# Reordering the first 16 microseconds: weight pieces between the input loads, an eviction moved up, a variance moved down

## The chip, the cores and the metric

The kernel runs on one core of one Trainium2 chip. The metric is device time in microseconds (us) of one execution; several executions give a median. Most executions of one kernel here agree within 0.3%, about 2.4 us. The change is about fractions of a microsecond at the very start of an 802 us kernel; the traces stamp each instruction to about 0.01 us. "Span" is the time from the first to the last instruction in a profiled execution; it is some 2 us shorter than the device time.

## The reference, cut to what matters

```python
def reference(A_x, A_wq, A_wk, A_wv, A_wo, A_beta, B_x, B_w_in, B_w_sp, B_b_sp, B_w_out):
    h = x + _A_ref(_layernorm(x), A_wq, A_wk, A_wv, A_wo, A_beta)   # segmented attention with a memory
    return h + _B_ref(_layernorm(h), B_w_in, B_w_sp, B_b_sp, B_w_out)  # gated MLP
```

x is 2048 x 1024 in bf16. The sequence is worked on in four segments of 512 tokens, each segment in four chunks of 128. Only the start matters here: the layernorm of the first segment's four chunks (0 to 3), their transposition, and the first projections with w_v, w_k and w_q.

## The kernel before: the parts that the change and the argument touch

All instructions go through a recorder that keeps the written order on each engine and sets the semaphores. So the order of the lines is the order on each engine.

For the first segment, only the mean is subtracted before the transposition. 1/std is applied later: to V when it leaves PSUM, where TensorE puts its results (`v_out`; such a copy out of PSUM is called an eviction), and to Q and K through a row vector RB, which TensorE makes with two matmuls of ones x diag(1/std). Those two matmuls need the 1/std of all four chunks. Variances come either from VectorE's statistics (chunks 0, 1, 2) or from a ScalarE pass over squares (chunk 3, `act_var`).

```python
    for tc in range(4):
        x_load(tc)
    for i in range(0, 8, 2):                      # w_v's first half in four pieces of 256 KB
        sp.dma_start(WV[0][:, i:i + 2, :], A_wv[...])
    sp.dma_start(WK[:, :, 0:256], ...)            # then w_k, beta, w_q, w_v's second half
    ...
    def act_mean(tc):    # ScalarE: MEAN[tc] = -sum(x) / D
    def act_var(tc):     # ScalarE: sum of (x - mean)^2; GpSimd adds eps
    def var0(k):         # GpSimd: variance from VectorE's statistics, plus eps
    def rstd0(tc):       # GpSimd: RS0[tc] = var ** -0.5
    def center(tc, m):   # VectorE: x - mean, in bf16
    def diag(tc):        # VectorE: two operations, diag(RS0[tc]) as a bf16 pair
    def pe_Th(tcl, src, e0, e1):  # TensorE: 8 transposes into 2 PSUM banks, evicted by engines e0 and e1
    ...
    warm(9)
    act_mean(1)
    var0(ln_stats(XCH[0]))
    c0 = center(0, MV[0][:, 0:1], ALU.subtract)
    c1 = center(1, MEAN[1][:])
    pe_Th(0, c0, dve, dve)
    act_mean(2)
    pe_Th(1, c1, act, dve)
    act_mean(3)
    rstd0(0)
    c2 = center(2, MEAN[2][:])
    var0(ln_stats(XCH[1]))
    rstd0(1)
    act_var(3)
    c3 = center(3, MEAN[3][:])
    warm(2)
    vb = [next_bank() for _ in range(2)]
    for i in range(5):
        for t in range(2):
            v_mm(0, t, 0, vb[t], i)      # V of chunks 0 and 1: needs chunk 0 and 1 transposed, and w_v
    pe_Th(2, c2, act, dve)
    rstd0(3)
    var0(ln_stats(XCH[2]))
    rstd0(2)
    diag(0)
    for i in range(5, 8):
        for t in range(2):
            v_mm(0, t, 0, vb[t], i)
    pe_Th(3, c3, act, dve)
    v_out(0, 0, 0, vb[0]); diag(1); diag(3); diag(2); v_out(0, 1, 0, vb[1])
    proj_v(0, 2, 0)
    ...
    mm8(bank(bk), WK ..., XNT[0] ...)             # first w_k projection
    for i in range(2):
        pe.matmul(bank(br), ONES[:], DIAG[i]...)  # ones x diag
    mm8(bank(bq), WQ ..., XNT[0] ...)             # first w_q projection
    for tc in range(4, 8):
        x_load(tc)
    sp.dma_start(WK[:, :, 256:D], ...)            # 1.5 MB
    sp.dma_start(WQ[:, :, 256:D], ...)            # 1.5 MB
    phi_exp(0); phi_max(0)                        # ends with the first transposed load, pk<-pqk
    ...
    def state(n):                                 # matmuls PK x V; state(0) needs the first pk
```

The softmax here doesn't subtract the row's maximum and nothing guards it: scores larger than these inputs give would overflow.

## Time and profile before

| | before |
|---|---|
| device time, median of 3 (range) | 802.45 us (801.4 to 803.39) |
| span of the profiled execution | 800.7 us |
| TensorE busy | 789.3 us (99%) |
| first w_v piece landed | 8.37 us |
| first w_q weight load | 16.52 us |

A page line "PE 789.3 (99%)" says that hardly anything is to be gained outside the places where TensorE stands still. These places are at the start. The next lines are from the timeline of the kernel before, TensorE's weight loads (PEld; PE are its matmuls, DVE is VectorE, ACT ScalarE, POOL GpSimd). The columns are start, time taken, engine, line, operation, out<-in, shapes and count; the brackets say how long the engine had idled and what ended it. I read weight loads rather than matmuls, since some matmul records are missing (this trace holds 15 of the first 16 V matmuls). A weight load starts up to 0.2 us ahead of its matmul: here transposes 3 are at 12.19 and 12.41.

```profile
5.79 0.90 PEld L209 LDWEIGHTS ps<-ident,lno 128*128 128x128 bf16 x16 [1.10 <-DVE lno L209]
...
8.48 1.85 PEld L209 LDWEIGHTS ps<-wv,xnT 128*128 128x128 bf16 x10 [1.68 <-DVE lno L209]
...
12.19 0.65 PEld L209 LDWEIGHTS ps<-ident,lno 128*128 128x128 bf16 x8
12.80 1.45 PEld L209 LDWEIGHTS ps<-wv,xnT 128*128 128x128 bf16 x8
14.37 1.61 PEld L209 LDWEIGHTS ps<-xnT,wk 128*128 128x128 bf16 x8
16.09 0.31 PEld L209 LDWEIGHTS ps<-diag,ones 128*128 128x128 bf16 x2
16.52 0.53 PEld L209 LDWEIGHTS ps<-xnT,wq 128*128 128x128 bf16 x3
```

No weight was loaded for 1.7 us ahead of the first V matmul at 8.48 (TensorE itself, which still worked on the two warm-up matmuls, stood for 1.2 us of that). The transposes of chunk 3 started at 12.19. From there to the first w_q weight load at 16.52, which I call "the tail", there is no bracket: TensorE was never held up. The tail is 16.52 - 12.19 = 4.33 us. The name in the 1.68 us bracket (DVE lno) is not the true releaser: lno was long written. The chain of waits of the same kernel (start, time taken, what) names it, and also shows what came next:

```profile
2.65 5.72 DMA wv<-in_A_wv_dram
8.37 0.14 issue
8.51 3.63 PE ps L209 x22
12.14 0.05 issue
12.19 8.30 PE ps L209 x44
20.49 10.24 DMA pk<-pqk
30.73 0.05 issue
30.78 0.41 PE ps L209 x4
```

TensorE waited for the w_v piece until 8.37, and the `state(0)` matmuls at 30.78 began as soon as pk had landed at 30.73. VectorE's timeline of the kernel before shows where the statistics of chunk 2 and the diag operations lay:

```profile
11.65 1.41 DVE L209 BATCH_NORM_STATS2 stats<-xch 128x6 f32<-128x512 bf16 x2
...
13.73 0.42 DVE L209 COPY xnT<-ps 128x512 bf16<-128x512 bf16 x1
...
15.46 0.35 DVE L209 SCALAR_TENSOR_TENSOR diag<-ident,rs,diag 128x128 bf16<-128x128 bf16 x1
```

The statistics ran ahead of chunk 3's copy (13.73), and the last diag operation ended at 15.81, before TensorE asked for it at 16.09.

### The profile page before, as it was taken

The page shows a single profiled execution, that of the slowest core. Times are in us where ns is not written, and L with a number is a line of the kernel's source. Part 1 is how long each engine was busy: PE and PEld are TensorE (multiplying, and loading weights), DVE is VectorE, ACT ScalarE, POOL GpSimd, SP SyncE. Part 2 cuts the span into 40 slices and gives each one's busy share as a digit, 9 for nine tenths or more (in the row PEclk, how much of TensorE's full clock was granted, in tenths as well). Part 3 has the DMA queues.
Part 4 walks back from the last instruction along what each step waited for, and adds up shares of the span by engine and source line. Part 5 has one row for each costly group of instructions (what it writes and reads, how often), then busy time and mean ns, then how long its engine had stood idle before and what let it go on. Part 6 is the DMA issues. An engine that isn't in the chain of part 4 may idle for free.

```text
span 800.7 us, 12419 instructions
## 1 busy us (share of the span) xinstructions
PE 789.3 (99%) x5301; PEld 380.0 (47%) x5371; DVE 379.2 (47%) x769; ACT 297.9 (37%) x347; POOL 129.0 (16%) x241
## 2 busy tenths in 40 slices
PE   8999999999999999999999999999999999999998
PEld 3445445555454445455544444444444444444444
DVE  6675688569853774844562000053234323323432
ACT  5777877877778675133333333100000000000000
POOL 4443333333333331100131000000000000000000
PEclk9999999999999999999999999999999999999999
DMA  9772535353516324611116000650270153021002
GB/s 292 176 164 56 93 81 119 87 102 83 99 31 126 113 54 100 170 47 53 53 53 132 1 0 1 203 107 6 80 132 1 33 110 75 0 66 47 1 7 86
DMA packets 125000, 64.79 MB, mean 81 GB/s; under 512 B 94992, under 2 KB 113936, under 8 KB 124944
## 3 DMA queue, kind: packets, MB, share of 16 engines
q1 hardware_dynamic: 124944, 63.99, 33.6%
q8 instruction: 42, 0.69, 0.4%
q14 instruction: 14, 0.11, 0.1%
HBM read 32.51 MB, written 8.39 MB: 51 GB/s over the span
## 4 chain that ended last, share of the span: by engine, by line
PE 94%; DVE 3%; DMA 2%; issue 1%; SPq 0%
PE ps L209 94%; DMA pk<-pqk 1%; DMA wv<-in_A_wv_dram 1%; DVE stats L209 1%; DVE ta L209 0%; DVE otok L209 0%; DVE hch L209 0%; SPq L209 0%; DVE rd L209 0%; DVE pqk L209 0%; DVE mzb L209 0%; DVE lno L209 0%; DVE rdm L209 0%; DVE msum L209 0%; DVE mv L209 0%
## 5 line engine op out<-in xcount | busy, mean ns | idle before, releaser
L209 PE MATMUL ps<-wspT,z 128*128 128x512 bf16 x878 | 193.1, 379 | 0.9
L209 ACT ACTIVATE e<-ps 128x2048 bf16<-128x2048 f32 (+1 forms) x96 | 152.8, 1592 | 49.5 <-PE ps L209 49.0
L209 PEld LDWEIGHTS ps<-wspT,z 128*128 128x128 bf16 x896 | 87.7, 98 | 105.7
L209 DVE TENSOR_TENSOR tmpg<-ps,brow 128x512 f32<-128x512 f32 x56 | 38.7, 691 | 197.0 <-DMA brow<-in_B_b_sp_dram 105.5
L209 POOL TENSOR_SCALAR_AFFINE_SELECT e<-e 128x512 bf16<-128x512 bf16 x128 | 83.9, 666 | 179.9 <-ACT e L209 179.8
L209 PE MATMUL ps<-win,hnT 128*128 128x448 bf16 x512 | 98.3, 352 | 0.0
L209 PE MATMUL ps<-w_out,yT 128*128 128x512 bf16 (+2 forms) x453 | 96.9, 372 | 0.5
L209 PE MATMUL ps<-hnT,win 128*128 128x512 bf16 x439 | 96.2, 379 | 0.5
L209 PEld LDWEIGHTS ps<-win,hnT 128*128 128x128 bf16 x512 | 49.8, 98 | 46.3 <-issue 0.2
L209 PEld LDWEIGHTS ps<-w_out,yT 128*128 128x128 bf16 x462 | 44.7, 98 | 52.4
L209 PEld LDWEIGHTS ps<-hnT,win 128*128 128x128 bf16 x448 | 43.9, 98 | 52.8
L209 PE MATMUL ps<-xnT,wk 128*128 128x512 bf16 x256 | 60.8, 380 | 0.0
L209 PE MATMUL ps<-wv,xnT 128*128 128x512 bf16 x254 | 58.8, 379 | 1.3 <-DMA wv<-in_A_wv_dram 1.2
L209 ACT ACTIVATE z<-ps 128x448 bf16<-128x448 f32 x60 | 32.5, 543 | 69.4 <-PE ps L209 69.4
L209 PE MATMUL ps<-wo,oT 128*128 128x512 bf16 x254 | 57.6, 379 | 0.1
L209 ACT ACTIVATE z1T<-ps 128x512 bf16<-128x512 f32 x56 | 33.4, 597 | 63.3 <-PE ps L209 63.3
L209 DVE TENSOR_TENSOR fin<-fin,ps 128x512 bf16<-128x512 bf16 (+2 forms) x33 | 22.2, 672 | 71.2 <-DMA fin<-out_dram 40.0
L209 PE MATMUL ps<-xnT,wq 128*128 128x512 bf16 x226 | 54.0, 379 | 1.6
L209 DVE BATCH_NORM_STATS2 zst<-z 128x6 f32<-128x448 bf16 x64 | 38.9, 620 | 30.1 <-ACT z L209 30.1
L209 PEld LDWEIGHTS ps<-v,e 128*128 128x128 bf16 x1280 | 37.3, 96 | 9.1 <-issue 1.7
L209 DVE TENSOR_TENSOR yT<-tmpg,z1T 128x512 bf16<-128x512 f32 x56 | 38.8, 692 | 1.9
L209 PE MATMUL ps<-v,e 128*128 128x33 bf16 x1280 | 38.4, 177 | 0.0
(83 smaller groups left out, 574.0 us busy)
## 6 DMA issues: line engine op xcount, KB each, us to landing
xch<-in_A_x_dram SPq DMA_DIRECT2D x16, 256.0 KB, 3.2
xr<-in_A_x_dram SPq DMA_DIRECT2D x16, 256.0 KB, 3.6
out_dram<-hch SPq DMA_DIRECT2D x16, 256.0 KB, 2.5
fin<-out_dram SPq DMA_DIRECT2D x16, 256.0 KB, 2.8
out_dram<-fin SPq DMA_DIRECT2D x31, 128.0 KB, 1.7
win<-in_B_w_in_dram SPq DMA_DIRECT2D x4, 896.0 KB, 5.3
w_out<-in_B_w_out_dram SPq DMA_DIRECT2D x1, 3584.0 KB, 13.6
win<-in_B_w_in_dram SPq DMA_DIRECT2D x3, 1024.0 KB, 5.4
```

Of the source, the lines that this page charges most:

```text
L209: ins = getattr(e, op.name)(*op.args, **op.kw)
```

## The change

The intent is to let the V matmuls start earlier. w_v's pieces come between the x chunks; ScalarE evicts chunk 1 before it works on chunk 2's mean; the two warm-up matmuls that filled the wait go. In exchange, chunk 3's variance (ScalarE) and, with it, chunk 2's statistics (VectorE) move behind chunk 3's transposes. The centering of chunk 2 (`c2`) also moves, behind chunk 1's statistics on VectorE.

```diff
-    for tc in range(4):
-        x_load(tc)
-    for i in range(0, 8, 2):
-        sp.dma_start(WV[0][:, i:i + 2, :],
-                     A_wv[i * 128:(i + 2) * 128, 0:512].rearrange("(c p) n -> p c n", p=128))
+    for k in range(8):
+        if k in (0, 1, 3, 5):
+            x_load((k + 1) // 2)
+        else:
+            i = {2: 0, 4: 2, 6: 4, 7: 6}[k]
+            sp.dma_start(WV[0][:, i:i + 2, :],
+                         A_wv[i * 128:(i + 2) * 128, 0:512].rearrange("(c p) n -> p c n", p=128))
@@
     pe_Th(0, c0, dve, dve)
+    pe_Th(1, c1, act, dve)
     act_mean(2)
-    pe_Th(1, c1, act, dve)
-    act_mean(3)
     rstd0(0)
-    c2 = center(2, MEAN[2][:])
     var0(ln_stats(XCH[1]))
     rstd0(1)
-    act_var(3)
-    c3 = center(3, MEAN[3][:])
-    warm(2)
+    c2 = center(2, MEAN[2][:])
+    act_mean(3)
     vb = [next_bank() for _ in range(2)]
-    for i in range(5):
+    for i in range(4):
         for t in range(2):
             v_mm(0, t, 0, vb[t], i)
     pe_Th(2, c2, act, dve)
+    c3 = center(3, MEAN[3][:])
+    for i in range(4, 8):
+        for t in range(2):
+            v_mm(0, t, 0, vb[t], i)
+    pe_Th(3, c3, act, dve)
+    act_var(3)
     rstd0(3)
     var0(ln_stats(XCH[2]))
     rstd0(2)
     diag(0)
-    for i in range(5, 8):
-        for t in range(2):
-            v_mm(0, t, 0, vb[t], i)
-    pe_Th(3, c3, act, dve)
     v_out(0, 0, 0, vb[0])
```

## The prediction

> **What bounds it.** Over the 800.7 us span TensorE is busy 99% (the page's part 1). The change touches the first 15 us alone. By the timeline, TensorE there waits until 5.80 us for the first transposes, and from 7.29 to 8.51 for the first w_v piece (the chain of waits: 5.72 us of "DMA wv", then TensorE until 20.49). Then the chain leaves TensorE: "DMA pk<-pqk" from 20.49 to 30.73, the transposed load that the first `state` matmuls wait for; they start at 30.78, when TensorE's previous work (logits) has just ended at 30.65. So TensorE has only some 0.1 us of slack against that landing.
>
> **What moves, costed from the trace.**
> Landings go by slot of 256 KB: 3.5, 4.2, 6.3, 7.7, 8.4, 9.1, 9.9 and 10.6 us. The Trainium skill (DMA: Bandwidth & Descriptors, "Queues, rings and completion order") says each engine consumes descriptors in ring order; the landings agree. The new order gives w_v piece 0 the 6.3 slot instead of 8.4, x2 7.7 instead of 6.3, piece 1 8.4, x3 9.1, pieces 2 and 3 still 9.9 and 10.6.
>
> - Chunk 1's ScalarE eviction (0.58 us) no longer stands behind mean 2 (1.06 + 0.19): it ends near 7.1 instead of 8.0. Two warm matmuls go.
> - V matmuls (0.22 us each) start near 7.2 instead of 8.5, stall about 0.3 us for piece 1, end their first eight near 9.3. Mean 2 runs 7.7–9.0, c2 ends 9.45; transposes 2 near 9.5; the next eight 9.9–11.65; transposes 3 11.65–12.1 instead of 12.4–12.85. `proj_v(0,2)` starts 0.75 us earlier, the w_k projection too, ending near 15.6 instead of 16.3.
> - But now variance 3 comes late: ScalarE does it after chunk 3's eviction, about 12.5–13.8 (before: 9.1–10.3), and VectorE's statistics of chunk 2 (1.41 + 0.21) stand behind chunk 3's copy, 12.5–14.1. GpSimd then makes the two rstd one after the other (0.2 + 0.6 each), ending near 15.6; the last diag pair ends near 16.2 (before 15.8). The ones×diag matmuls, which started at 16.31, will wait for it, and start at about 16.25. So nearly all of the 0.75 us is given back there: instead of a wait for w_v, a wait of about 0.6 us for diag.
>
> **On the critical path.** At the ones×diag matmuls I expect 0 to 0.2 us gain (a loss of up to 0.4 is possible). Anything that remains ends at `state(0)`: the pk landing hangs behind w_k and w_q (3 MB), in a stream that runs at 350–390 GB/s from 14 to 26 us (the same page puts the HBM limit of a core near 358; the trace is slightly above it). The same bytes go out in the same time, so pk lands near 30.7 whatever TensorE did before. Net effect: about 0.
>
> **Predicted:** 802.5 us, range 801.3 to 803.6 (8 in 10; mostly the spread of the runs, 801.4 to 803.4). Chances: faster by over 2% 0.005, within 2% 0.985, slower by over 2% 0.01.
>
> **Would show it right:** first V matmul at 7.1–7.5 us; transposes 3 at 11.5–12; a new TensorE wait of about 0.6 us on DVE diag before the ones×diag matmuls, which start at 16.1–16.5; `state(0)` at 30.6–30.9, with TensorE's part of the wait on DMA pk unchanged or slightly longer; the rest of the trace shifted by less than 0.3 us.
>
> **Would make it wrong:** the dip of the load stream at 3.5–5 us (74–213 GB/s) vanishing or growing with the new order, which would move all landings, pk too; GpSimd's rstd ops faster or slower than 0.6 us; w_v piece 0 or x2 landing over 1 us off their slots; x loads 6 and 7, which now wait for later readers, delaying w_k and w_q so far that the stream runs dry.

## The result, and the profile after

| | before | after |
|---|---|---|
| device time, median of 4 (range) | 802.57 us (801.4 to 803.39) | 802.28 us (801.98 to 802.58) |
| ratio, 95% interval | | 0.9997 (0.998 to 1.0015) |
| span of the profiled execution | 800.66 us | 800.25 us |
| first w_v piece landed | 8.37 us | 5.99 us |
| transposes of chunk 3 | 12.19 us | 11.21 us |
| first w_q weight load | 16.52 us | 16.30 us |
| first pk landed | 30.73 us | 29.62 us |

A ratio is the mean time of one kernel's fast runs over that of the other's fast runs of the same rounds, so it is not quite the ratio of the medians. The timeline of the kernel after, weight loads, answers the lines of before:

```profile
6.64 0.10 PEld L209 LDWEIGHTS ps<-wv,xnT 128*128 128x128 bf16 x1
7.25 0.33 PEld L209 LDWEIGHTS ps<-wv,xnT 128*128 128x128 bf16 x3 [0.52 <-ACT xnT L209]
...
9.23 0.45 PEld L209 LDWEIGHTS ps<-ident,lno 128*128 128x128 bf16 x8 [0.78 <-DVE lno L209]
...
11.21 0.65 PEld L209 LDWEIGHTS ps<-ident,lno 128*128 128x128 bf16 x8
11.81 1.45 PEld L209 LDWEIGHTS ps<-wv,xnT 128*128 128x128 bf16 x8
13.38 1.61 PEld L209 LDWEIGHTS ps<-xnT,wk 128*128 128x128 bf16 x8
15.89 0.10 PEld L209 LDWEIGHTS ps<-diag,ones 128*128 128x128 bf16 x1 [0.91 <-DVE diag L209]
16.28 0.10 PEld L209 LDWEIGHTS ps<-diag,ones 128*128 128x128 bf16 x1 [0.29 <-DVE diag L209]
16.30 0.75 PEld L209 LDWEIGHTS ps<-xnT,wq 128*128 128x128 bf16 x4
```

The V matmuls start at 6.64 instead of 8.48, 1.84 us earlier, and the transposes of chunk 3 are 0.98 us earlier. Much of the difference is the wait of 0.78 us at 9.23: the transposes of chunk 2 now wait for VectorE, which centers chunk 2 behind chunk 1's statistics. No run moved that operation back. But the tail now has a wait in it, named DVE diag, and takes 16.30 - 11.21 = 5.09 us instead of 4.33. So 0.76 of the 0.98 us are given back. VectorE's timeline of the kernel after shows what the wait is made of:

```profile
12.07 0.42 DVE L209 COPY xnT<-ps 128x512 bf16<-128x512 bf16 x1 [1.35 <-PE ps L209]
12.41 1.41 DVE L209 BATCH_NORM_STATS2 stats<-xch 128x6 f32<-128x512 bf16 x2
13.86 0.21 DVE L209 BATCH_NORM_AGGREGATE mv<-stats 128x2 f32<-128x12 f32 x1
13.98 0.20 DVE L209 TENSOR_SCALAR diag<-ident,rs 128x128 bf16<-128x128 bf16 x1
...
15.88 0.35 DVE L209 SCALAR_TENSOR_TENSOR diag<-ident,rs,diag 128x128 bf16<-128x128 bf16 x1
```

VectorE idles 1.35 us ahead of chunk 3's copy. Only then come the statistics (1.6 us with the aggregate) and the eight diag operations (2.25 us), one after the other without a gap, to 16.23.

The weight loads of `state(0)` (first line before, second after; each from its own timeline) answer to the chain's pk step:

```profile
30.78 0.23 PEld L209 LDWEIGHTS ps<-v,pk 128*128 128x128 bf16 x4 [0.41 <-DMA pk<-pqk]
```

```profile
30.35 0.23 PEld L209 LDWEIGHTS ps<-v,pk 128*128 128x128 bf16 x4 [0.21 <-issue]
```

After, pk landed 1.1 us earlier and nothing waited for it. I had said that it would land at the same time.

### The profile page after: what moved, and what is told of

Read it like the earlier page. It is cut to its first block, busy times and chain, and to the rows that moved or that the text cites. A ratio compares the mean times of both kernels' runs of the same rounds, so it can differ in the third digit from the quotient of the medians.

```text
span 800.3 us, 12483 instructions
## 1 busy us (share of the span) xinstructions
PE 793.6 (99%) x5369; PEld 379.8 (47%) x5369; DVE 379.5 (47%) x769; ACT 297.9 (37%) x347; POOL 129.2 (16%) x241
## 4 chain that ended last, share of the span: by engine, by line
PE 95%; DVE 4%; ACT 0%; issue 0%
PE ps L209 95%; DVE stats L209 1%; ACT e L209 0%; DVE ta L209 0%; DVE otok L209 0%; DVE hch L209 0%; DVE diag L209 0%; DVE rd L209 0%; DVE xnT L209 0%; DVE pqk L209 0%; DVE lno L209 0%; DVE mv L209 0%; DVE mzb L209 0%; DVE etmp L209 0%; DVE rdm L209 0%
## 5 line engine op out<-in xcount | busy, mean ns | idle before, releaser
L209 PE MATMUL ps<-xnT,wq 128*128 128x512 bf16 x256 | 60.5, 379 | 0.0
```

Of the source, the lines that this page charges most:

```text
L209: ins = getattr(e, op.name)(*op.args, **op.kw)
```

## The experiments

Twelve runs were made: eight (a profile and one time each) and five rounds of four kernels. All results were correct. Here is what all fourteen traces show. Times are us from the start of the span; the transposes, w_q and `state(0)` are the starts of their weight loads; "tail" is w_q minus transposes 3; "clock" is the moment from which the trace's clock record has TensorE's full clock; "rest" is span minus w_q.

| run | loads / engines | clock | w_v piece landed | transposes 3 | w_q | tail | pk landed | state(0) | span | rest |
|---|---|---|---|---|---|---|---|---|---|---|
| before | old / old | 4.47 | 8.37 | 12.19 | 16.52 | 4.33 | 30.73 | 30.78 | 800.66 | 784.14 |
| b_rep | old / old | 5.52 | 7.64 | 11.46 | 15.79 | 4.33 | 29.78 | 29.84 | 799.70 | 783.91 |
| b_r5 | old / old | 5.25 | 7.40 | 11.27 | 15.60 | 4.33 | 29.74 | 29.78 | 799.67 | 784.08 |
| after | new / new | 5.86 | 5.99 | 11.21 | 16.30 | 5.09 | 29.62 | 30.35 | 800.25 | 783.96 |
| a_rep | new / new | 4.62 | 6.63 | 11.35 | 16.43 | 5.08 | 29.18 | 30.49 | 800.35 | 783.92 |
| a_r5 | new / new | 5.89 | 6.27 | 11.33 | 16.42 | 5.09 | 29.07 | 30.48 | 800.36 | 783.94 |
| loads_only | new / old | 5.30 | 5.84 | 12.12 | 16.45 | 4.33 | 28.74 | 30.51 | 800.38 | 783.93 |
| engines_only | old / new | 6.41 | 7.83 | 11.65 | 16.74 | 5.09 | 29.07 | 30.80 | 800.66 | 783.92 |
| a_var3 | new / new, variance 3 early | 5.07 | 5.01 | 11.41 | 16.50 | 5.09 | 28.65 | 30.56 | 800.42 | 783.92 |
| a_stats2 | new / new, statistics 2 early | 5.07 | 5.64 | 11.21 | 16.33 | 5.12 | 30.41 | 30.46 | 800.35 | 784.02 |
| a_both | new / new, both early | 5.84 | 5.55 | 11.24 | 15.57 | 4.33 | 29.75 | 29.79 | 799.66 | 784.09 |
| a_both_r5 | the same | 6.82 | 6.17 | 11.70 | 16.03 | 4.33 | 29.43 | 30.08 | 799.98 | 783.95 |
| a_both_pk | both early, pk before w_q's rest | 7.45 | 5.73 | 12.03 | 16.36 | 4.33 | 24.51 | 30.42 | 800.29 | 783.93 |
| a_both_pk_r5 | the same | 4.46 | 5.92 | 11.30 | 15.63 | 4.33 | 24.87 | 29.69 | 799.75 | 784.12 |

The last column is the key to the table. Behind the first w_q matmul all kernels are alike: 783.91 to 783.96 us, or up to 0.2 us more where something still held TensorE near `state(0)`. So span = transposes 3 + tail + rest, and each of the three terms can be looked at alone.

### The kernel before, again (b_rep)

Its edit is nothing: it asks how far the trace of before repeats.

> The kernel before, unchanged, for the scatter of single stamps. If traces repeat: first V matmul 8.5 us, transposes of chunk 3 at 12.4, ones x diag at 16.3, first w_q matmul 16.7 (each within 0.15), w_q's rest lands at 29.5 and the first pk at 30.7, state(0) at 30.8. Theory A (the 0.2 us at state(0) is a wait on pk that lands late because of the load order): pk again after 30.5. Rival B (pk's landing varies by a us from run to run, whatever the order): pk may land anywhere from 29.5 to 31, and state(0) then starts at 30.6 without a wait in some runs.

Measured: 801.42 us (before on the same chip: 802.26), span 799.70. It did not repeat. The w_v piece landed at 7.64, and everything behind it was 0.73 us earlier up to w_q. The timeline, weight loads:

```profile
7.75 1.85 PEld L209 LDWEIGHTS ps<-wv,xnT 128*128 128x128 bf16 x10 [0.87 <-DVE xnT L209]
...
11.46 0.65 PEld L209 LDWEIGHTS ps<-ident,lno 128*128 128x128 bf16 x8
...
15.79 1.18 PEld L209 LDWEIGHTS ps<-xnT,wq 128*128 128x128 bf16 x6
```

and the step of its chain of waits that stands where before had 5.72 us:

```profile
2.65 4.99 DMA wv<-in_A_wv_dram
```

The same load, issued at the same moment, took 4.99 instead of 5.72 us. Between 4 and 5 us the load stream moved 152 GB/s in the first profile of before and 254 in this one (windows view). So the trace that I had predicted from held a slow draw of a load, and the size of the possible gain was read from that draw. Theory A, that the load order fixes pk's landing, also fell here: pk landed at 29.78 with the old order.

### The changed kernel, again (a_rep)

> The changed kernel, unchanged, for the scatter. If traces repeat: first V matmul 6.6 us, transposes of chunk 3 at 11.4, ones x diag 15.9, first w_q matmul 16.5, state(0) 30.4. Theory A: pk lands again near 29.6, before TensorE needs it. Rival B: it may land as late as 30.7, and state(0) then waits until then.

Measured: 802.06 us, span 800.35. This one repeats: w_q at 16.43 against 16.30, although the piece landed 0.64 us later than in the first trace. The V matmuls start at 6.78 and 6.64: set by the transposes, not by the load. pk landed at 29.18 and was not waited for.

### The new loads alone (loads_only)

```diff
 before, with the new order of the eight loads; the engines' order is untouched
```

> Only the new order of loads; all engines in the order of before. First V piece lands near 6.0, x2 near 6.8 (0.5 later than before). ScalarE still does mean 2 before chunk 1's eviction, so that ends near 8.6 and the V matmuls start near 8.7, 0.2 later than before: the piece that landed early is of no use. My theory (TensorE's start is set by the later of piece and eviction, so both parts of the change are needed): transposes of chunk 3 at 12.5-12.8, first w_q matmul 16.7-17.0. Rival (the loads alone bring the gain): V matmuls before 7.7 and w_q before 16.5. Theory A of pk: pk lands near 29.6 as in the changed kernel; rival B: no telling.

Measured: 802.10 us, span 800.38. The piece landed at 5.84, but only the first V matmul used it. Its timeline, weight loads:

```profile
6.77 0.10 PEld L209 LDWEIGHTS ps<-wv,xnT 128*128 128x128 bf16 x1
8.64 1.62 PEld L209 LDWEIGHTS ps<-wv,xnT 128*128 128x128 bf16 x9 [1.77 <-ACT xnT L209]
```

The second V matmul needs chunk 1, which ScalarE still evicts behind mean 2; it waited until 8.64 for it. The expectation for that (near 8.7) was right. The expected stamps are those of matmuls: transposes 3 were expected at 12.5 or later and started at 12.34, the first w_q matmul at 16.7 or later and started at 16.67. The rival's w_q before 16.5 did not come. Of the V matmuls, which it had before 7.7, only the first started so early. Against the two repeats of before, w_q is 0.66 and 0.85 us later. So the loads alone bring nothing, and against a quick draw of before they cost.

### The new engine order alone (engines_only)

```diff
 after, with the old order of the eight loads
```

> Only the new order on the engines; loads as before. Chunk 1 is evicted by 7.2, but the V matmuls wait for the first piece until about 8.4-8.5. Then eight matmuls, transposes 2 near 10.3, transposes 3 near 12.4, and behind them variance 3 (to 14.5), statistics of chunk 2 (to 15), diag (to 17.2): ones x diag at 16.9, first w_q matmul at 17.4-17.6, that is 0.7-0.8 later than before, and state(0) near 31.4. Rival (the late variance and statistics cost nothing, as TensorE has other work): w_q at 16.7 or earlier. Theory A of pk: pk lands near 30.7 with the old loads, too early to matter here.

Measured: 802.38 us, span 800.66. The piece landed at 7.83, earlier than the 8.4 to 8.5 that I had counted on, and the absolute times are earlier by about as much (first w_q matmul 16.95 instead of 17.4 to 17.6). Against its own transposes the result is clear:

```profile
11.65 0.65 PEld L209 LDWEIGHTS ps<-ident,lno 128*128 128x128 bf16 x8
...
16.34 0.10 PEld L209 LDWEIGHTS ps<-diag,ones 128*128 128x128 bf16 x1 [0.90 <-DVE diag L209]
```

The tail is 5.09 us, as in the changed kernel, and has the same wait. In b_rep and here transposes 3 start 3.82 us after the piece has landed, so with the landing taken out the new engine order costs the tail's 0.76 us and gains nothing by itself. Only with both parts do transposes 3 stop following the landing: in after, a_rep and a_r5 they start at 11.21 to 11.35, with the piece landing at 5.99 to 6.63.

### Which of the two moved operations makes the wait (a_var3, a_stats2, a_both)

The changed kernel is edited in three ways: variance 3 alone put ahead of chunk 3's transposes, statistics 2 alone, and both.

```diff
-    pe_Th(3, c3, act, dve)
     act_var(3)
     rstd0(3)
+    pe_Th(3, c3, act, dve)          # a_var3
     var0(ln_stats(XCH[2]))
```

```diff
+    k2 = ln_stats(XCH[2])           # a_stats2
     pe_Th(3, c3, act, dve)
     act_var(3)
     rstd0(3)
-    var0(ln_stats(XCH[2]))
+    var0(k2)
```

a_both has `act_var(3); rstd0(3); k2 = ln_stats(XCH[2])` ahead of `pe_Th(3, ...)`.

> The changed kernel with variance 3 put back ahead of chunk 3's eviction (ScalarE is idle from 10.3 to 11.8 there, and it takes 1.24 us). Theory C (the diag chain is held at two places at once: VectorE's statistics of chunk 2 behind chunk 3's copy, and variance 3): no gain from this alone, since VectorE still reaches diag 0 at 14.0 and ends the eight diag operations at 16.2: ones x diag at 15.9, w_q at 16.5, both within 0.1 of the changed kernel. Rival D (the late variance is the whole cost, as the change's words suggest): ones x diag at 15.3, w_q at 15.75.

> The changed kernel with the statistics of chunk 2 put ahead of chunk 3's copy on VectorE (idle there from 10.7 to 12.1; they take 1.63 us, so the copy comes 0.25 later). Theory C: no gain from this alone either: diag 0 and 1 are done by 13.9, but diag 3 waits for variance 3 (rstd ready near 14.5) and diag 2 for the rstd that GpSimd makes after it (15.5): ones x diag near 15.9, w_q 16.4-16.6. Rival E (VectorE's statistics are the whole cost): ones x diag at 15.3, w_q at 15.75.

> Both moves. Theory C: the wait on diag is gone, w_k's projection runs straight into ones x diag at 15.3 and w_q at 15.75, 0.75 earlier than the changed kernel and 1.0 than before. state(0) would be free at 29.6. If pk lands at 29.6 as in the changed kernel it starts at 29.6-29.8; if pk's landing is set by the load stream and lies at 30.7, it starts there and 1 us of the gain is lost (theory of my prediction). Rival F (the w_k and w_q pieces or something else holds TensorE there too): w_q at 16.3 or later with another engine or a load named in the wait.

Measured: a_var3 802.14 us, tail 5.09; a_stats2 802.07 us, tail 5.12; a_both 801.38 us, tail 4.33. Either move alone gains nothing, both together gain the whole 0.76 us. The two rivals that blamed one operation fell. In a_var3 VectorE still works from 12.61 to 16.43 without a gap. In a_stats2 VectorE is early and waits for GpSimd instead, whose 1/std of chunks 3 and 2 stand behind the late variance. VectorE's timeline of a_stats2:

```profile
13.33 0.35 DVE L209 SCALAR_TENSOR_TENSOR diag<-ident,rs,diag 128x128 bf16<-128x128 bf16 x1
14.52 0.25 DVE L209 TENSOR_SCALAR diag<-ident,rs 128x128 bf16<-128x128 bf16 x1 [0.84 <-POOL rs L209]
...
15.62 0.26 DVE L209 TENSOR_SCALAR diag<-ident,rs 128x128 bf16<-128x128 bf16 x1 [0.46 <-POOL rs L209]
```

Two chains end at the same moment, and each covers the other. In a_both VectorE's idle time ahead of chunk 3's copy is filled with the statistics (10.66 to 12.32), and no line has a bracket. VectorE's statistics and copy, then TensorE's weight loads, of a_both:

```profile
10.66 1.42 DVE L209 BATCH_NORM_STATS2 stats<-xch 128x6 f32<-128x512 bf16 x2
...
12.24 0.37 DVE L209 COPY xnT<-ps 128x512 bf16<-128x512 bf16 x1
```

```profile
11.24 0.65 PEld L209 LDWEIGHTS ps<-ident,lno 128*128 128x128 bf16 x8
...
15.14 0.31 PEld L209 LDWEIGHTS ps<-diag,ones 128*128 128x128 bf16 x2
15.57 1.39 PEld L209 LDWEIGHTS ps<-xnT,wq 128*128 128x128 bf16 x7
```

The first w_q matmul, some 0.2 us behind its weight load, started at 15.79; 15.75 was expected. At `state(0)` pk landed at 29.75 and held TensorE for about 0.17 us (rest 784.09 against 783.92). So a kernel that is early enough does meet pk, as b_r5 does too (784.08).

### pk ahead of w_q's remainder (a_both_pk)

```diff
-    sp.dma_start(WQ[:, :, 256:D], wcols(A_wq, 256, D))
     phi_exp(0)
     phi_max(0)                       # issues the transposed load of pk
+    sp.dma_start(WQ[:, :, 256:D], wcols(A_wq, 256, D))
```

> Both moves, and the load of w_q's remaining 1.5 MB issued after the first transposed load of pk and not before it. If pk queues behind those bytes (1.5 MB at about 370 GB/s is 4.1 us, an estimate), it lands near 25-26.5 instead of 29.6-30.7, and state(0) starts at 29.6 without a wait. The rest of w_q then lands near 29.5-30.5, and its first use (third head group, near 30) may wait for it: up to 0.5 us. Rival (pk's landing has another cause, such as the transposed mode itself): still 29.5 or later.

Measured: pk landed at 24.51 instead of 29.75, w_q's remainder at 28.73, and `state(0)` did not wait. That pk queues behind those 1.5 MB is shown. Here is the load of pk in the two kernels' DMA views (kind, count, us from issue to landing), before first, then a_both_pk:

```profile
pk<-pqk SPq DMA_TRANSPOSE x1, 10.2
```

```profile
pk<-pqk SPq DMA_TRANSPOSE x1, 4.2
```

But the execution was slow at another place: 802.00 us, w_q at 16.36. Its 16 first transposes took 1.85 us. Here are the TensorE lines of the two executions of this one kernel, a_both_pk first, then a_both_pk_r5:

```profile
5.77 1.85 PE L209 MATMUL ps<-ident,lno 128*128 128x128 bf16 x16 [0.15 <-DVE lno L209]
```

```profile
5.82 1.07 PE L209 MATMUL ps<-ident,lno 128*128 128x128 bf16 x16 [0.71 <-DVE lno L209]
```

In the first the clock record shows TensorE's full clock only from 7.45 us on, in the second from 4.46. The Trainium skill (TensorE: Matmul & The Clock Gate, "Part 1: The HAM clock gate") says that the array runs at half clock until a free-running window has seen enough activity, and calls the moment run-variable. The traces agree that the moment varies; the window itself no run here shows. The same code differs by 0.78 us in these transposes, which start 0.106 us apart in the first and 0.056 us apart in the second, and by 0.73 us at transposes 3 (12.03 against 11.30). In a_both_r5 the full clock came at 6.82 and transposes 3 start at 11.70, against 11.24 in a_both. With the old loads such a delay can hide behind the wait for the piece: in engines_only the full clock came at 6.41, and transposes 3 still follow the landing by 3.82 us.

### Timed: five rounds of four kernels (b_r5, a_r5, a_both_r5, a_both_pk_r5)

> The kernel before against itself, the noise floor of the timing: ratio 1.000 within 0.002. In the trace the first w_v piece lands between 7.6 and 8.4, the transposes of chunk 3 start 3.8 us after that landing, ones x diag 3.9 us after those, and the span is 783.9 us longer than the start of w_q's first weight load, plus any wait on pk at state(0). The times should scatter by about 1 us, as this landing does (before so far 801.4 to 803.4).

> The changed kernel. Ones x diag starts 4.68 us after the transposes of chunk 3, as in the five traces so far with this tail. w_q's first weight load at 16.3-16.5 where the full clock was granted before 6 us; if it is granted as late as 7.4, the transposes and the first V matmuls take up to 0.8 us longer and w_q comes near 17. Ratio to before 0.998 to 1.001; no difference of over 0.2%. If before's scatter comes from the landing of w_v alone, this kernel's times scatter less than before's.

> Both moves, timed. Theory: ones x diag 3.90 us after the transposes of chunk 3; 0.6 to 0.8 us less than the changed kernel and 0.2 to 1.0 less than before, that is a ratio to before near 0.9993 (0.998 to 1.000). Too small to be called faster; the trace decides. Rival (the gain is an accident of one trace): same mean as the changed kernel.

> Both moves, and pk ahead of w_q's rest. pk lands near 24.5 again and state(0) never waits; the rest of w_q lands before its use. If the earlier look of this kernel was slow because the full clock came only at 7.45 us in that execution, and not because of its code, w_q's first weight load is at 15.6-15.8 where the clock comes before 6 us, and the mean is 0 to 0.2 us below that of both moves. Rival (the code itself makes the transposes slow): 16 transposes take 1.8 us again with the clock granted early.

| run | median, us (range of 5) | ratio to before, 95% interval |
|---|---|---|
| before (shared runs, 9) | 801.72 (800.98 to 802.25) | |
| b_r5 | 801.40 (801.22 to 801.86) | 0.9997 (0.9985 to 1.0010) |
| a_r5 | 802.16 (801.93 to 802.85) | 1.0008 (0.9995 to 1.0020) |
| a_both_r5 | 801.49 (801.36 to 801.69) | 0.9998 (0.9984 to 1.0012) |
| a_both_pk_r5 | 801.48 (801.35 to 802.58) | 1.0000 (0.9988 to 1.0013) |

All intervals contain 1, so no kernel is faster or slower by the timing. On this chip the five times of the changed kernel lie above all five of b_r5 and above all five of a_both_r5, but not above all nine of the shared before. The medians of a_r5 and b_r5 differ by 0.76 us, their spans by 0.69 us, which the traces account for: w_q 0.82 us later (16.42 against 15.60), less the 0.14 us by which b_r5's rest is longer.

My expectation that the changed kernel's times would scatter less than before's was not borne out: its five range over 0.92 us, those of b_r5 over 0.64 and the nine shared ones of before over 1.27. In b_r5 the piece landed at 7.40, just outside the 7.6 to 8.4 that I had expected. Reordering pk did not help either. In a_both_pk_r5 pk is not waited for, but the rest is still 784.12: the matmuls of w_q's remainder, which landed at 29.98, start at 30.08. By the times of the landing and the start the wait moved from pk to w_q, as the expectation had allowed for. The profile names another releaser for those last 0.16 us, so this is argued and not shown.

No version beats both kernels: a_both is 0.67 us below the changed kernel (801.49 against 802.16) and level with before.

## Why the prediction was right or wrong

**The time: right.** 802.5 us predicted, 802.28 measured. That says little of the mechanism: executions of before alone lie between 801.4 and 803.39 us, far wider apart than what was at stake. Of the landmarks that were to show the prediction right, most were missed: the first V matmul (6.64 instead of 7.1 to 7.5), the matmuls of transposes 3 (11.42 instead of 11.5 to 12), the first of the two ones x diag matmuls (15.90 instead of 16.1 to 16.5; the second came at 16.29) and `state(0)`. That TensorE gained about 0.2 us at w_q, the upper end of "0 to 0.2", is in part luck, as the first failed step below shows.

**"w_v piece 0 in the 6.3 slot, x2 in 7.7": roughly right.** 5.99 and 6.81 us, and the landings follow the order of issue. The Trainium skill (DMA: Bandwidth & Descriptors, "Queues, rings and completion order") says that descriptors, the pieces that a load is cut into, are consumed in ring order on each engine. The traces agree as far as they show it: in all fourteen the loads of the first 20 us land in the order of issue, though at other moments in each.

**"V matmuls start near 7.2", transposes 3 at 11.65: right in mechanism.** They started at 6.64 and 11.21. Only the second V matmul needs ScalarE's eviction, and that one came at 7.25.

**"Nearly all of the 0.75 us is given back" at diag: right.** 0.76 us were given back: the tail is 5.08 to 5.12 instead of 4.33 us in all traces with the new engine order and neither or one of the repairs, and 4.33 again with both. I had named GpSimd's last 1/std as the end of the chain. In the changed kernel VectorE's own chain sets the end: it has no gap from 12.41 to 16.23, so it never waited there for GpSimd, whose last 1/std ended at 15.55. With the statistics moved (a_stats2) GpSimd's chain ended at nearly the same moment; the experiments with one repair show that each alone is enough for the whole loss.

**The step that failed first: "instead of 8.5" and "0.75 us earlier".** This term of the sum was read from one trace, in which the w_v piece landed late, at 8.37 us. In two more traces of the same kernel it landed at 7.64 and 7.40, and transposes 3 started at 11.46 and 11.27. Against those the change starts transposes 3 only 0.25 and 0.06 us earlier (11.21), and by its 0.76 us longer tail it starts w_q 0.51 and 0.70 us later (16.30). So whether the change gains 0.22 us or loses 0.7 depends on a draw of before.

**The step that failed second: "pk lands near 30.7 whatever TensorE did before", with `state(0)` at 30.6 to 30.9.** pk landed at 29.62 and `state(0)` began at 30.35. In the twelve traces that issue w_q's remainder first, pk landed anywhere from 28.65 to 30.73, with either order of the loads. Right was the mechanism: pk queues behind those bytes, as the reordering showed (24.51 and 24.87 us), and a kernel that is early meets it (a_both, b_r5). Wrong was to take one landing for a constant. The prediction had itself named what would move all landings, pk too: a change of the dip in the load stream near 3.5 to 5 us. That is what the traces show, but not as an effect of the new order, since b_rep has it with the old one. The windows view from 4 to 5 us (the last two numbers are the DMA share and GB/s) of before, after and b_rep:

```profile
4.00:5.00 1.00, 1.00 (x5) 0.25 (x2) 0.94 (x2) 0.82 (x1) 0.00 (x0) 1.00 0.77 152
```

```profile
4.00:5.00 1.00, 1.00 (x4) 0.31 (x3) 0.93 (x3) 0.95 (x1) 0.00 (x0) 1.00 1.07 276
```

```profile
4.00:5.00 1.00, 1.00 (x4) 0.30 (x2) 0.97 (x2) 0.76 (x1) 0.00 (x0) 1.00 0.76 254
```

In the same order, the first w_k load, issued at 4.67 in all three, landed at 12.44, 11.71 and 11.67, w_q's remainder at 29.47, 28.60 and 28.51, and pk at 30.73, 29.62 and 29.78. So most of pk's 1.1 us was there by the first w_k load (0.73) and w_q's remainder (0.87), and both failed steps were read from one slow stream in the trace of before. What remains is the lag of pk behind w_q's remainder, 0.4 to 1.3 us in the twelve traces. It goes with how early pk was issued: 1.26 or 1.27 us where that was 8.8 to 9.0 us ahead of the remainder's landing, 0.40 to 0.43 where it was 7.8 to 8.1. No run tested this, and its cause stays open.

**Open:** what makes the loads of the first microseconds quicker or slower from one execution to the next, and whether the two removed warm-up matmuls matter. They were not tested alone. What they could do for the clock is small by the traces: they stood behind the 16 first transposes, and in thirteen traces the full clock came before the last of these transposes started (in a_both_pk 0.11 us after it, at 7.45). In all fourteen it then stayed full until after the last matmul, with the two matmuls or without.

## What to carry to other kernels

Before reading a gain from a wait for a load, take the trace of the unchanged kernel a second time: here TensorE's wait for the w_v piece, which the change was made for, was 1.2 us in one execution and 0.4 and 0.3 us in the next two (waits view). When work is moved out of the way of an early stage, look up who needs its result next, and put it into an idle stretch of its engine rather than behind the stage; if two moved operations feed the same consumer, undoing one of them can show nothing. In a kernel whose later part is the same to 0.05 us, split the span at a landmark (transposes 3, w_q) and compare the pieces: that resolves tenths of a microsecond which five rounds of timing do not.

## What the Trainium skill lacked or had wrong

- TensorE: Matmul & The Clock Gate, "Part 1: The HAM clock gate", gives ±500 ns from run to run for the moment at which the full clock comes, around 4 us into sustained matmuls. (It also calls the moment run-variable, but with counts of matmuls and no range in us.) Fourteen traces here, all with the first matmul at 1.6 to 1.75 us, have it from 4.46 to 7.45 us, which are also the two moments of one kernel (a_both_pk and its repeat), a range of 3 us; in one execution that cost 0.78 us in 16 transposes. The matmuls ahead of it were not quite unbroken: in a_both_pk they paused for 0.15 us.
- DMA: Bandwidth & Descriptors gives no scatter for the landing of one and the same load at the start of a kernel. The first w_v piece, issued at 2.65 us in three traces of one kernel, landed at 8.37, 7.64 and 7.40 us.
- The same page gives no delay for a transposed load that is issued behind a backlog of plain loads on the same queue: pk landed 8.2 to 10.3 us after its issue near 20 us with 1.5 MB more ahead of it, and 4.2 and 5.3 us after it without them.
